# Sliding-window attention and a hard-swish MLP on one core: batch 0's values loaded by heads, w_out whole ahead of batch 1, seven units ahead of its stage

## The chip, the cores and the metric

The kernel runs on one core of a Trainium2 chip. A core has TensorE (PE in the profile; its weight loads are PEld), VectorE (DVE), ScalarE (ACT), GpSimd (POOL) and SyncE (SP); they run side by side and wait for one another by semaphores. DMAs are issued by POOL or SP and move data between the chip's memory (HBM) and the on-chip memory SBUF. PE writes to PSUM, eight banks of 2 KB a partition. The metric is the device time of one execution in microseconds; a profiled execution gives a span from the first to the last instruction, and some time lies around it.

## The reference

For 8 batches, 8 heads, 576 positions and a head size of 64, causal attention over a window of 64 positions; then, with the heads side by side as 512 columns and all batches as 4608 rows, an MLP with hidden size 2048:

```
scores = q @ k.T / 8                      # masked to 0 <= i - j < 64
attn   = softmax(scores);  o = attn @ v
x      = o as (4608, 512)
h      = x @ w_in                          # (4608, 2048)
g      = h * clip(h + 3, 0, 6) / 6
out    = g @ w_out                         # (4608, 512), float32
```

All inputs are float32 in HBM; the kernel computes in bf16 and accumulates in float32. The loads cast to bf16 on the way.

## The kernel before

The program is written out by hand under a manual schedule: each engine executes its instructions in the order in which the code issues them, and a wait at the head of an engine's queue holds everything behind it on that engine. Semaphores are placed by the framework from the tiles read and written.

The heads are worked in pairs, so a step t stands for one pair g of one batch b (t = 4b + g). Per pair the kernel transposes q and k on PE, copies them out of PSUM (KT for the keys, QZ or Q for the queries), forms scores, takes exp on ACT, multiplies with the values (P·V), scales by the reciprocals of the sums, transposes the result and copies it into xT, the left operand of the MLP. The MLP runs over blocks of 512 rows: 16 "first units" (fc 0 to 15, four matmuls with w_in each, one for each pair, L485; then ACT L497 and DVE L498 make gT) and 16 "second units" (four matmuls with w_out each, L521; four units make 128 rows of the output, copied by ACT at L527 and stored by SP).

Batch 0 has a path of its own, the head of the program:
- load_early_qk (L107) loads q and k pair by pair; load_early_v (L126) loads the values in five pieces of 128 rows with all heads (the last has 64 rows). Both are issued by POOL, which also sets up the identity and the window masks (window, late_windows) and issues w_in (three parts: fc 0 to 3, 4 to 7, 8 to 15, L163), w_out (two halves, L169), batch 1's q and k (L118) and its values (L137).
- t_k and t_q transpose a pair's keys and queries, 12 PE instructions each. The keys are copied by DVE (L239), the queries half by ACT and half by DVE (L231). The DVE half waits for the ACT half.
- s0_ makes a pair's scores with the mask added on PE (L248, L251), in three PSUM tiles of the pool ps_t, which has three banks; ACT takes the exp of each (L259 twice, L265).
- Vs is the value tile shifted by 64 rows; shift_early(m) makes it from Vn, two copies for each piece m of 128 rows, the first two pieces on POOL and the others on DVE (L150, L152).
- pv_early is P·V, 20 matmuls (L354), then a reciprocal (L363) and a product (L364) on DVE into opg. x_early transposes opg on PE (L375, five, into a tile of ps_t) and ACT copies it to xT (L378).
- warm issues matmuls on zeros that nothing reads.
- The first units of block 0 begin before all pairs are there: u(fc, gs) does the matmuls of the pairs gs and keeps the bank half way; inputs does so for several fc; complete adds the last pair and finishes fc 0 to 4.

After the head, the rest of block 0's first units runs (44 matmuls of the remaining fc), and then the 16 second units of block 0 are used as filling work: weave(n) executes the next n units of the queue moe. Between them stands batch 1's front: turn_two(4) and then, for t = 4 to 7, turn (36 transposes, L276), s_first and s_rest (scores), and weights (exp on ACT, product with the window on DVE). Then come pv and pv_out of t = 4 to 7, x_turned, batch 2's first loads, turn_two(8) and the first units of block 1. From batch 2 on a regular loop (group) weaves the MLP units between the attention steps.

POOL's DMAs use eight completion semaphores in turn, so the issue of a DMA waits until the eighth DMA before it has landed.

Of the kernel before, what the change touches and what calls it, by code (L numbers as in the profile page):

```python
# [24 lines left out]
P = 128  # L25
D = 64
W = 64
# [9 lines left out]
def kernel(  # L37
# [60 lines left out]
    def load_early_qk(pairs, first=0):  # L98
        if first:
            tiles = staged[0]  # L100
        else:
            both = stage.tile([SP, 2, H, R * D], BF16, name="qk6", tag="qk")
            tiles = [both[:, 0], both[:, 1]]
        h = 2 * first
        for n in pairs:
            for t, src in zip(tiles, (q, k)):
                nc.gpsimd.dma_start(  # L107
                    out=t[:, h : h + 2 * n, :],
                    in_=src[0, h : h + 2 * n].rearrange("h (p r) d -> p h (r d)", r=R),
                )  # L110
            h += 2 * n
        return tiles

    def load_qk(b, n=NG, first=0):
        t = staged[b] if first else stage.tile([P, H, RL * D], BF16, name="qk9", tag="qk")
        hs = slice(2 * first, 2 * (first + n))
        for z, src in enumerate((k, q)):
            nc.gpsimd.dma_start(  # L118
                out=t[halves[z], hs], in_=src[b, hs].rearrange("h (p r) d -> p h (r d)", r=RL)
            )  # L120
        return t

    def load_early_v():
        for m in range(NM):
            n = min(P, S - m * P)
            nc.gpsimd.dma_start(  # L126
                out=Vn[0][:n, m, :, 0:D], in_=v[0, :, m * P : m * P + n, :].rearrange("h s d -> s h d"),
            )

    def load_v(b, whole=False, part=slice(None)):  # L130
# [13 lines left out]
            memset(t[:, :, :, 0:VO], 1.0)  # L144
            memset(t[:, :, :, VO + P : VW], 1.0)

    def shift_early(m, move):

        vn, vs = Vn[0], Vs[0]
        move(out=vs[W:P, m], in_=vn[0:W, m])  # L150
        if m + 1 < NM:
            move(out=vs[0:W, m + 1], in_=vn[W:P, m])  # L152

    def shift(b):

# [4 lines left out]
    def load_w_in(i):  # L160
        n = FF // 4
        c = (slice(0, n), slice(n, 2 * n), slice(2 * n, FF))[i]
        nc.gpsimd.dma_start(  # L163
            out=win16[:, :, c], in_=moe_w_in[:, c].rearrange("(g p) f -> p g f", p=P)
        )

    def load_w_out(c):
        n = NFC // 2
        nc.gpsimd.dma_start(  # L169
            out=wout16[:, c * n : (c + 1) * n, :],  # L170
            in_=moe_w_out[c * n * P : (c + 1) * n * P, :].rearrange("(c p) j -> p c j", p=P),
        )
# [13 lines left out]
    def window():  # L186

        for sign, base in ((-1, -1), (1, W)):
            nc.gpsimd.affine_select(
                out=outside[:], in_=outside[:], pattern=[[sign, W]], compare_op=ISGE,  # L190
                fill=-BIG, base=base, channel_multiplier=-sign,
            )
# [15 lines left out]
    def zero_rows(i):  # L208
        nc.vector.memset(KT[i][:, 0:W], 0.0)
        nc.vector.memset(QZ[i][D:P, 0, :], 0.0)  # L210
        nc.vector.memset(QZ[i][0:D, 1, :], 0.0)
# [32 lines left out]
    def s0_(t):  # L244

        kt, qz = KT[t % 4], QZ[t % 4]
        def window_scores(to, w):
            nc.tensor.matmul(  # L248
                to, lhsT=ident[:], rhs=outside[:].unsqueeze(1).to_broadcast([P, 2, W]), start=True, stop=False
            )  # L250
            nc.tensor.matmul(  # L251
                to, lhsT=kt[:, w * W : w * W + P], rhs=qz[:, :, w * W : (w + 1) * W], start=False, stop=True
            )

        for a in range(2):
            sc = ps_t.tile([P, 2, NM - 1, W], F32, name="sc", tag="bk")
            for m in range(NM - 1):
                window_scores(sc[:, :, m], 2 * m + a)
            nc.scalar.activation(  # L259
                out=Pz[t % 4][:, :, :, a].rearrange("p h m w -> p (h m) w"),  # L260
                in_=sc[:].rearrange("p h m w -> p (h m) w"), func=EXP, scale=scale,
            )
        sl = ps_t.tile([P, 2, W], F32, name="sl", tag="bk")
        window_scores(sl[:], NW - 1)
        nc.scalar.activation(out=Pl[t % 4][:, :, 0:W], in_=sl[:], func=EXP, scale=scale)  # L265
# [73 lines left out]
    def pv_early(t):  # L339
        b, g = divmod(t, NG)  # L340
        vn, vs, pz, pl = Vn[b % 2], Vs[b % 2], Pz[t % 4], Pl[t % 4]
        if t in (1, 3):
            os = [ps_h.tile([P, 1, 512], F32, name="oh", tag="bk") for _ in range(2)]
        else:
            os = [ps_o.tile([P, 2, 512], F32, name="o", tag="o")]
        n = len(os)
        for h in range(2):
            hh = 2 * g + h
            o = os[h % n][:, h // n]
            for m in range(NM):  # L350
                om = o[:, m * (D + 1) : (m + 1) * (D + 1)]
                for a in range(2):
                    last = m == NM - 1
                    nc.tensor.matmul(  # L354
                        om[a * W : (a + 1) * W], lhsT=pl[:, h, a * W : (a + 1) * W] if last else pz[:, h, m, a, :],
                        rhs=(vn if a and not last else vs)[:, m, hh, 0 : D + 1], start=True, stop=True,
                    )
        opg = work.tile([P, NM, 2, D], BF16, name="opg")
        for i, o in enumerate(os):
            hs = slice(i, i + 2 // n)  # L360
            ov = o[:, :, 0 : NM * (D + 1)].rearrange("p h (m c) -> p h m c", c=D + 1)
            rec = recs[:, t, hs, 0:NM]
            nc.vector.reciprocal(out=rec.unsqueeze(3), in_=ov[:, :, :, D : D + 1])  # L363
            nc.vector.tensor_tensor(  # L364
                out=opg[:, :, hs].rearrange("p m h d -> p h m d"), in0=ov[:, :, :, 0:D],
                in1=rec.unsqueeze(3).to_broadcast([P, 2 // n, NM, D]), op=MULT,
            )
        opgs[t] = opg
# [202 lines left out]
    def weave(n):  # L571
        for _ in range(min(n, len(moe))):
            moe.popleft()()
# [98 lines left out]
    )  # L672
    load_early_qk((1,), 1)
    window()
    load_early_qk((1,) * (NG - 2), 2)
    zero_rows(0)
    nc.vector.memset(Vn[0][:, :, :, D:VC], 1.0)
    nc.vector.memset(band[:], 1.0)
    nc.vector.memset(first[:], 1.0)
    pads(1, nc.vector.memset)  # L680
    load_early_v()
    nc.vector.memset(Vs[0][0:W, 0], 0.0)
    for i in range(2):
        load_w_in(i)
    for m in range(2):
        shift_early(m, nc.gpsimd.tensor_copy)
    load_w_in(2)
    late_windows()
    load_w_out(0)
    staged[1] = load_qk(1, 2)  # L690
    load_w_out(1)
    load_qk(1, 2, 2)
    load_v(1, True)
    nc.vector.memset(recs[:], 1.0)
# [14 lines left out]
    t_q(1)  # L709
    zero_rows(3)  # L710
    s0_(0)
    t_k(2)
    t_q(2)
    s0_(1)
    t_k(3)
    t_q(3)
    s0_(2)
    for m in range(2, NM):
        shift_early(m, nc.vector.tensor_copy)
    s0_(3)  # L720
    warm(ps_acc, 4)
    pv_early(0)
    pv_early(1)
    warm(ps_acc, 2)
    x_early(0)
    pv_early(2)
    queue_block(0, 0)
    u = units[0][0]

    def inputs(gs, fcs, **to):  # L730
        for fc in fcs:
            u(fc, gs, **to)

    u(0, (0,), ps_acc)
    inputs((0,), (1, 2), pool=ps_t)
    x_early(1)
    pv_early(3)
    x_early(2)
    inputs((1,), range(3))
    for fc, to in zip((3, 4), pair_bank()):  # L740
        u(fc, (0, 1), to=to)
    x_early(3)
    inputs((2,), range(5))
    complete(0, range(5), (3, 4))
    def group(t, n):

        if t >= 2 * NG:
            pv(t)
        if t + 2 < T:
            turn(t + 2)  # L750
        if t + 1 < T:
            host = t + 2
            if host >= T:
                hosts[host] = [ps_h.tile([P, 8 * P], BF16, name=name, tag="bk") for name in ("tk", "tq")]
            s = s_first(t + 1, host)
            weights(t + 1, s, s_rest(t + 1))
        if t >= 2 * NG:
            pv_out(t)
        if t + 2 < T:
            turned(t + 2, 0)  # L760
        if t >= 2 * NG:
            x_(t)
        weave(2)
        if t + 2 < T:
            turned(t + 2, 1)
        weave(n - 2)
# [16 lines left out]
    n = NG  # L783
# [6 lines left out]
            (3, 0), (3, 1), (3, 2), (3, 3),  # L790
        )
    )
    weave(2)
    turn_two(n)
    weave(2)
    for t in range(n, n + 4):
        if t < n + 3:
            turn(t + 1)
        s = s_first(t, min(t + 1, n + 3))

        def copies():
            if t < n + 3:
                turned(t + 1, 0)
                turned(t + 1, 1)

        weights(t, s, s_rest(t), own, copies)
        if t < n + 3:
            weave((4, 2, 2)[t - n])
    nc.gpsimd.tensor_copy(out=seen[:], in_=P0[(n + 3) % 4][0:1, 0, 0, 0:1])
    staged[2] = load_qk(2, 1)  # L810
    for t in range(n, n + 4):
# [82 lines left out]
```

## Time and profile before

| what | value |
|---|---|
| median of 3 runs | 322.94 us (322.43 to 323.59) |
| profiled execution | 323.23 us, span 321.5 us |
| busy in the span | PE 307.6 us (96%), ACT 183.9 (57%), DVE 177.6 (55%), POOL 125.3 (39%) |
| granted TensorE clock, mean | 0.993 |
| HBM read and written | 37.62 and 9.44 MB |
| PE busy, 5 to 10, 10 to 15, 15 to 20, 20 to 25 us | 3.82, 4.34, 4.14, 4.42 of 5.00 us each |
| PE busy, 25 to 45 us | 20.00 of 20.00 us |
| DMA, 15 to 30 us | 208 GB/s |

Times in the profile's lines are microseconds from the span's start, then the duration; "L126" is line 126 of the kernel; "x5" counts instructions; a bracket names the idle time of the engine just before and what ended it. In the groups the columns are busy time and the mean duration of one in ns, then idle time before them and its main releaser. A busy PE is not PE at its peak: matmuls overlap in the pipeline, and a 128x512 one that lasts 379 ns is followed by the next after 216 ns.

### The profile page before, as it was taken

How to read it: one execution, taken by the hardware profiler on the slowest of the kernel's cores; microseconds unless marked ns; L12 is line 12 of the kernel's file. 1: busy time of each engine (PE TensorE's matmuls, PEld its weight loads, DVE VectorE, ACT ScalarE, POOL GpSimd, SP SyncE). 2: the span in 40 equal slices, each digit the busy share in tenths (PEclk: the TensorE clock that was granted, in tenths of full speed). 3: DMA queues.
4: the chain of work that ended last, by engine and by line, in shares of the span. 5: the costliest groups of instructions: out<-in, count | busy, mean ns of one | idle time of the engine just before them, and what ended most of it. 6: DMA issues, size and time to landing. Idle time of an engine off the chain costs nothing.

```text
span 321.5 us, 11140 instructions
## 1 busy us (share of the span) xinstructions
PE 307.6 (96%) x4824; PEld 156.0 (49%) x4824; DVE 177.6 (55%) x385; ACT 183.9 (57%) x345; POOL 125.3 (39%) x171
## 2 busy tenths in 40 slices
PE   7889999999989999999999999999999999999992
PEld 3744454545544555555555555555544444444440
DVE  7876757488446743775377527762676156334200
ACT  2737665598457764776477547763774356455310
POOL 8991204587866335553455335633330000000000
PEclk9999999999999999999999999999999999999997
DMA  6999995979979942994299349933022200100021
GB/s 86 169 211 206 208 184 112 220 103 115 198 103 167 123 117 86 164 130 117 87 157 136 108 97 149 147 102 103 6 62 42 86 33 0 65 35 34 34 74 66
DMA packets 57592, 35.67 MB, mean 111 GB/s; under 512 B 39872, under 2 KB 51648, under 8 KB 57536
## 3 DMA queue, kind: packets, MB, share of 16 engines
q0 software_dynamic: 35904, 18.81, 45.1%
q1 hardware_dynamic: 21632, 16.08, 21.2%
q8 instruction: 39, 0.64, 0.8%
q14 instruction: 17, 0.14, 0.1%
HBM read 37.62 MB, written 9.44 MB: 146 GB/s over the span
## 4 chain that ended last, share of the span: by engine, by line
PE 87%; ACT 3%; DVE 2%; POOL 2%; DMA 2%; issue 2%; POOLq 0%; ACTq 0%; DVEq 0%
PE hT L485 37%; PE acc L521 37%; PE o L403 4%; PE s L310 2%; PE acco L521 2%; DMA V<-in_v_dram 2%; PE tk L276 2%; POOL qk L107 2%; ACT t L497 1%; DVE gT L498 1%; PE tq L276 1%; POOL V L126 1%; PE hTo L485 1%; PE xp L375 0%; ACT e L323 0%
## 5 line engine op out<-in xcount | busy, mean ns | idle before, releaser
L498 DVE SCALAR_TENSOR_TENSOR gT<-t,hT 128x512 bf16<-128x512 bf16 x141 | 95.8, 687 | 82.7 <-ACT t L497 82.2
L485 PE MATMUL hT<-xT,win 128*128 128x512 bf16 x564 | 133.2, 379 | 1.5 <-DVE gT L498 0.6
L521 PE MATMUL acc<-wout,gT 128*128 128x512 bf16 x544 | 129.1, 379 | 0.0
L497 ACT ACTIVATE t<-hT,half_const 128x512 bf16<-128x512 f32 x141 | 95.8, 689 | 51.1 <-PE hT L485 50.5
L485 PEld LDWEIGHTS <-win 128*128 128x128 bf16 x576 | 55.8, 98 | 67.6 <-issue 2.6
L521 PEld LDWEIGHTS <-gT 128*128 128x128 bf16 x576 | 54.3, 98 | 62.8
L331 POOL TENSOR_TENSOR Pz<-e,band 128x512 bf16<-128x512 bf16 x48 | 54.1, 1145 | 0.0
L328 POOL TENSOR_TENSOR P<-e,first 64x256 bf16<-64x256 bf16 x24 | 15.9, 662 | 86.8 <-ACT e L319 86.8
L527 ACT COPY osb<-acc 128x512 f32<-128x512 f32 x34 | 19.9, 586 | 43.9 <-PE acc L521 41.1
L323 ACT ACTIVATE e<-s 128x512 bf16<-128x512 f32 x56 | 30.1, 592 | 0.0
L283 DVE COPY KT<-tk 128x576 bf16<-128x576 bf16 x28 | 20.8, 743 | 5.3 <-ACT e L319 4.5
L137 POOL DMA_DIRECT2D V<-in_v_dram x22 | 18.0, 821 | 8.3 <-DMA wout<-in_moe_w_out_dram 4.2
L412 DVE TENSOR_REDUCE sums<-o 128x12 f32<-128x24 f32 x26 | 4.6, 179 | 27.6 <-PE o L403 27.6
L403 PEld LDWEIGHTS <-Pz 64*64 64x64 bf16 x1120 | 13.5, 108 | 13.0 <-issue 11.6
L426 DVE TENSOR_TENSOR opl<-o,recs 128x256 bf16<-128x256 f32 x52 | 19.2, 406 | 0.0
L283 ACT COPY QZ<-tq 128x576 bf16<-128x576 bf16 x28 | 17.8, 637 | 1.5 <-PE tq L276 1.5
L403 PE MATMUL o<-V,Pz 64*64 64x65 bf16 x1040 | 15.5, 195 | 0.8 <-issue 0.8
L319 ACT ACTIVATE e<-tk 64x128 bf16<-64x128 f32 x28 | 7.6, 270 | 13.9 <-PE tq L296 13.9
L310 PE MATMUL s<-QZ,KT 64*64 64x64 bf16 x896 | 14.4, 195 | 0.4 <-DVE gT L498 0.4
L276 PE MATMUL tk<-ident,qk 64*64 64x64 bf16 x504 | 13.9, 195 | 0.0
L276 PE MATMUL tq<-ident,qk 64*64 64x64 bf16 x504 | 13.9, 195 | 0.0
L276 PEld LDWEIGHTS <-qk 64*64 64x64 bf16 x1008 | 11.5, 106 | 2.3 <-issue 2.1
(102 smaller groups left out, 209.0 us busy)
## 6 DMA issues: line engine op xcount, KB each, us to landing
out_dram<-osb SPq DMA_DIRECT2D x36, 256.0 KB, 2.2
V<-in_v_dram POOLq DMA_DIRECT2D x16, 256.0 KB, 6.2
V<-V SPq DMA_DIRECT2D x6, 432.0 KB, 5.0
qk<-in_k_dram POOLq DMA_DIRECT2D x4, 576.0 KB, 6.4
qk<-in_q_dram POOLq DMA_DIRECT2D x4, 576.0 KB, 9.2
wout<-in_moe_w_out_dram POOLq DMA_DIRECT2D x2, 1024.0 KB, 15.6
qk<-in_q_dram POOLq DMA_DIRECT2D x12, 144.0 KB, 4.5
qk<-in_k_dram POOLq DMA_DIRECT2D x12, 144.0 KB, 4.3
```

The source lines that it names most:

```text
L276: nc.tensor.transpose(out=hosts[t][z][halves[h], r * W : (r + 1) * W], in_=staged[b][halves[z], 2 * g + h, r * D : (r + 1) * D], identity= ...
L283: (nc.scalar.copy if z else nc.vector.tensor_copy)(out=(QZ[t % 4][:, 0] if z else KT[t % 4][:, W:]).rearrange("q (p r) -> q p r", r=RL), i ...
L310: nc.tensor.matmul(ss[h][halves[i], c, m, r], lhsT=keys(t, h, W * (w - 1), r), rhs=QZ[t % 4][halves[h], 0, w * W : (w + 1) * W], start=Tru ...
L323: nc.scalar.activation(out=e[:].rearrange("p c m r w -> p (c m r w)"), in_=ss[h][:].rearrange("p c m r w -> p (c m r w)"), func=EXP, scale ...
L331: muls[h].tensor_tensor(out=Pw[t % 4][:, h].rearrange("p c m r w -> p (c m) (r w)"), in0=e[:].rearrange("p c m r w -> p (c m) (r w)"), in1 ...
L403: nc.tensor.matmul(o[i][halves[c], c0 : c0 + D + 1], lhsT=p, rhs=vt[:, 2 * g + h, v0 : v0 + D + 1], start=(r == 0), stop=(r == 1), skip_gr ...
L426: nc.vector.tensor_tensor(out=opg[:, :, i], in0=ov[i][:, 2:6, 1 : D + 1].rearrange("p (m h) d -> p m h d", h=2), in1=rec[:, i, 2:6].rearra ...
L485: nc.tensor.matmul(hT, lhsT=win16[:, g, fc * P : (fc + 1) * P], rhs=xT[:, g, t0 : t0 + TB], start=(g == 0), stop=(g == NG - 1),)
L497: nc.scalar.activation(out=t1[:], in_=hT, func=RELU, bias=half_const[:], scale=1.0 / 6.0)
L498: nc.vector.scalar_tensor_tensor(out=gT[:, fc, :], in0=t1[:], scalar=1.0, in1=hT, op0=MIN, op1=MULT)
L521: nc.tensor.matmul(acc, lhsT=gT[:, fc, ts * P : (ts + 1) * P], rhs=wout16[:, fc, :], start=(fc == 0), stop=(fc == NFC - 1),)
L527: nc.scalar.copy(out=osb[:], in_=acc)
```

## The change

Batch 0's values are loaded by heads: load_early_v(heads) issues one DMA for each head given, with the rows 0 to 511 in four groups of 128, and load_early_v() one DMA for the last 64 rows of all heads. On POOL the order is now q and k of pairs 0 and 1, the window selects, the values of heads 0 to 3, the tail, q and k of pairs 2 and 3, the values of heads 4 to 7, the three parts of w_in, the late window selects, both halves of w_out, batch 1's q and k, its values. The number of DMAs for the values goes from five to nine.

shift_early takes a pair in place of a piece of rows: two copies of 64 partitions with 720 and 576 columns for each pair, pairs 0 and 2 on DVE, pairs 1 and 3 on ACT, none on POOL.

The order of the head becomes: transposes 0 and 1, scores 0, scores 1, shifts 0 and 1, P·V 0, transposes 2, P·V 1, scores 2, x_early 0, transposes 3, x_early 1, scores 3, shifts 2 and 3, P·V 2 and 3, x_early 2, and then the first units for fc 0 to 4 with pairs 0 and 1 together, pair 2, x_early 3 and the rest. Six warm matmuls go. P·V of pair 1 uses the pool ps_o in place of ps_h.

Of block 0's second units seven are executed before turn_two(4), one behind it, two, two and one in batch 1's rounds; before it was two, two and four, two, two. The three between the P·V steps stay, and the one that was left behind turn_two(8) is used up earlier.

```diff
@@ -120,11 +120,15 @@
             )
         return t
 
-    def load_early_v():
-        for m in range(NM):
-            n = min(P, S - m * P)
+    def load_early_v(heads=()):
+        whole = S - S % P
+        for h in heads:
             nc.gpsimd.dma_start(
-                out=Vn[0][:n, m, :, 0:D], in_=v[0, :, m * P : m * P + n, :].rearrange("h s d -> s h d"),
+                out=Vn[0][:, 0 : NM - 1, h, 0:D], in_=v[0, h, 0:whole].rearrange("(m p) d -> p m d", p=P)
+            )
+        if not heads:
+            nc.gpsimd.dma_start(
+                out=Vn[0][0 : S - whole, NM - 1, :, 0:D], in_=v[0, :, whole:S].rearrange("h s d -> s h d")
             )
 
     def load_v(b, whole=False, part=slice(None)):
@@ -144,12 +148,12 @@
             memset(t[:, :, :, 0:VO], 1.0)
             memset(t[:, :, :, VO + P : VW], 1.0)
 
-    def shift_early(m, move):
+    def shift_early(g, move):
 
         vn, vs = Vn[0], Vs[0]
-        move(out=vs[W:P, m], in_=vn[0:W, m])
-        if m + 1 < NM:
-            move(out=vs[0:W, m + 1], in_=vn[W:P, m])
+        hs = slice(2 * g, 2 * g + 2)
+        move(out=vs[W:P, :, hs], in_=vn[0:W, :, hs])
+        move(out=vs[0:W, 1:NM, hs], in_=vn[W:P, 0 : NM - 1, hs])
 
     def shift(b):
 
@@ -339,7 +343,7 @@
     def pv_early(t):
         b, g = divmod(t, NG)
         vn, vs, pz, pl = Vn[b % 2], Vs[b % 2], Pz[t % 4], Pl[t % 4]
-        if t in (1, 3):
+        if t == 3:
             os = [ps_h.tile([P, 1, 512], F32, name="oh", tag="bk") for _ in range(2)]
         else:
             os = [ps_o.tile([P, 2, 512], F32, name="o", tag="o")]
@@ -672,23 +676,22 @@
     )
     load_early_qk((1,), 1)
     window()
+    load_early_v(range(NG))
+    load_early_v()
     load_early_qk((1,) * (NG - 2), 2)
+    load_early_v(range(NG, H))
     zero_rows(0)
     nc.vector.memset(Vn[0][:, :, :, D:VC], 1.0)
     nc.vector.memset(band[:], 1.0)
     nc.vector.memset(first[:], 1.0)
     pads(1, nc.vector.memset)
-    load_early_v()
     nc.vector.memset(Vs[0][0:W, 0], 0.0)
-    for i in range(2):
+    for i in range(3):
         load_w_in(i)
-    for m in range(2):
-        shift_early(m, nc.gpsimd.tensor_copy)
-    load_w_in(2)
     late_windows()
     load_w_out(0)
+    load_w_out(1)
     staged[1] = load_qk(1, 2)
-    load_w_out(1)
     load_qk(1, 2, 2)
     load_v(1, True)
     nc.vector.memset(recs[:], 1.0)
@@ -709,21 +712,24 @@
     t_q(1)
     zero_rows(3)
     s0_(0)
+    s0_(1)
+    shift_early(0, nc.vector.tensor_copy)
+    shift_early(1, nc.scalar.copy)
+    pv_early(0)
     t_k(2)
     t_q(2)
-    s0_(1)
+    pv_early(1)
+    s0_(2)
+    x_early(0)
     t_k(3)
     t_q(3)
-    s0_(2)
-    for m in range(2, NM):
-        shift_early(m, nc.vector.tensor_copy)
+    x_early(1)
     s0_(3)
-    warm(ps_acc, 4)
-    pv_early(0)
-    pv_early(1)
-    warm(ps_acc, 2)
-    x_early(0)
+    shift_early(2, nc.vector.tensor_copy)
+    shift_early(3, nc.scalar.copy)
     pv_early(2)
+    pv_early(3)
+    x_early(2)
     queue_block(0, 0)
     u = units[0][0]
 
@@ -731,17 +737,15 @@
         for fc in fcs:
             u(fc, gs, **to)
 
-    u(0, (0,), ps_acc)
-    inputs((0,), (1, 2), pool=ps_t)
-    x_early(1)
-    pv_early(3)
-    x_early(2)
-    inputs((1,), range(3))
+    u(0, (0, 1), ps_acc)
+    inputs((0, 1), (1, 2), pool=ps_t)
     for fc, to in zip((3, 4), pair_bank()):
         u(fc, (0, 1), to=to)
+    inputs((2,), range(3))
     x_early(3)
-    inputs((2,), range(5))
+    inputs((2,), (3, 4))
     complete(0, range(5), (3, 4))
+
     def group(t, n):
 
         if t >= 2 * NG:
@@ -790,9 +794,9 @@
             (3, 0), (3, 1), (3, 2), (3, 3),
         )
     )
-    weave(2)
+    weave(7)
     turn_two(n)
-    weave(2)
+    weave(1)
     for t in range(n, n + 4):
         if t < n + 3:
             turn(t + 1)
@@ -805,7 +809,7 @@
 
         weights(t, s, s_rest(t), own, copies)
         if t < n + 3:
-            weave((4, 2, 2)[t - n])
+            weave((2, 2, 1)[t - n])
     nc.gpsimd.tensor_copy(out=seen[:], in_=P0[(n + 3) % 4][0:1, 0, 0, 0:1])
     staged[2] = load_qk(2, 1)
     for t in range(n, n + 4):
```

## The prediction

> **What bounds the kernel now.** I read the page first (shares, chain, groups), then the chain in order of time, then the timelines of the engines over the first 26 us, then the landing of each early DMA, last a table of busy time by stretch.
>
> ```profile
> PE 87%; ACT 3%; DVE 2%; POOL 2%; DMA 2%; issue 2%; POOLq 0%; ACTq 0%; DVEq 0%
> L485 PE MATMUL hT<-xT,win 128*128 128x512 bf16 x564 | 133.2, 379 | 1.5 <-DVE gT L498 0.6
> ```
>
> PE carries 87% of the chain and the big matmuls hardly wait. A change can only gain where PE is not yet dense, and it loses whatever delays the point from which PE is dense. The chain in order of time gives that point:
>
> ```profile
> 9.21 5.97 DMA V<-in_v_dram
> ...
> 16.31 0.60 DVE V L150
> ...
> 17.72 0.39 PE o L354 x11
> ...
> 19.76 0.65 ACT xT L378
> ...
> 26.66 9.50 PE hT L485 x44
> 36.15 1.73 PE acc L521 x8
> ```
>
> So today the head waits for batch 0's values (landed at 15.2), shifts them, runs the first P·V at 17.7, and from about 25.4 PE is dense: the 44 matmuls L485 end at 36.1, 0.216 us each. In the PE timeline the first matmul with w_in stands at 20.45 and the first L521 at 35.99; I count in those starts.
>
> What the head consists of, from the timelines of ACT, DVE and POOL:
>
> ```profile
> 9.88 1.08 ACT L259 ACTIVATE Pz<-sc 128x512 bf16<-128x512 f32 x2
> 10.85 0.29 ACT L265 ACTIVATE Pl<-sl 128x128 bf16<-128x128 f32 x1
> 14.11 0.76 DVE L231 COPY QZ<-tp 64x576 bf16<-64x576 bf16 x1
> 15.28 0.30 DVE L150 COPY V<-V 64x576 bf16<-64x576 bf16 x1 [0.41 <-DMA V<-in_v_dram]
> 15.62 0.66 DVE L152 COPY V<-V 64x576 bf16<-64x576 bf16 x1
> 18.39 0.82 DVE L364 TENSOR_TENSOR opg<-o,recs 128x640 bf16<-128x640 f32 x1
> 19.76 0.64 ACT L378 COPY xT<-xp 128x576 bf16<-128x576 bf16 x1 [3.00 <-PE xp L375]
> 7.45 4.22 POOL L126 DMA_DIRECT2D V<-in_v_dram  x5
> 26.57 0.88 POOL L137 DMA_DIRECT2D V<-in_v_dram  x1 [2.67 <-DMA win<-in_moe_w_in_dram]
> ```
>
> Today all four pairs' scores are finished (last L265 ends at 16.76) before the values are usable. Scores hide behind the load of V.
>
> **The change, step by step.**
>
> *Loads.* After the two window selects POOL is free at 5.0. Today q and k of pairs 2 and 3 follow (0.63 us each). Now four value loads (heads 0 to 3), the tail of 64 rows, those q and k, and four more value loads. One value load has 512 runs, like the tail of today, which took 0.73 (the whole ones 0.90). Heads 0 to 3 are issued from 5.0 to 7.92, the tail from 7.92, q2 8.65, k2 9.28, q3 9.91, k3 10.54, heads 4 to 7 from 11.2, w_in from 14.1 (11.6 today). Landing takes 3.4 (first) to 4.7 for q and k and 5.2 to 6.0 for V; I take 4.4, as of the q that now stands fifth, since the queue is less full. The tail lands at 12.3, k2 at 13.7, k3 at 14.9, heads 6 and 7 by 17.8. Each of these DMAs waits for the eighth before it (the 26.57 row is such a wait, on the third w_in load); all those have landed in time. w_in's first part lands at about 20.1 instead of 18.6, the second at 22.7 (21.2), the third at 27.8 (26.3); w_out whole at 37.7 (39.5), batch 1's q and k at 40.5 and 43.3 (34.6 and 42.5), its values near 48 either way. SP issues nothing here.
>
> *Head.* PE, ACT and DVE each keep the written order, and the order now interleaves scores and P·V. Scores 0 stay where they are; scores 1 move up and end on ACT at 12.8. From there, by the rows above:
> - DVE shifts pair 0 (720 and 576 columns) once the tail is there. A 576-column copy took 0.30 alone and 0.60 to 0.66 beside POOL, so 0.7 to 1.5 for two; POOL issues throughout, I take 1.0: 12.35 to 13.35.
> - P·V 0 on PE 0.55 (13.9); reciprocal and product on DVE 1.07 (18.14 to 19.21 today): 15.0.
> - Transposes of pair 2 stand behind P·V 0 on PE (14.65). Their two DVE copies (0.76 each) stand behind the product: 15.0 to 16.55. Today they ended at 13.29.
> - Scores 2 start at 16.6; today's scores 0 needed 1.13 from their first use of Q to the first exp's end and 1.85 to the last. The first exp ends at 17.75 and frees the bank that x_early(0) waits for; pair 3's transposes are queued behind it, to 18.75, though k3 landed at 14.9.
> - ACT finishes the last exp (18.45), copies xT 0 (0.6) and half of Q 3 (0.6): 19.65. DVE's half, which waits for it, ends at 20.45 (14.87 today).
> - Scores 3: 20.5, last exp at 22.35. Only then ACT shifts pair 3, two copies of about 0.65 (as L231, 0.63): 23.65. No row has ACT on this copy; 1.0 to 1.6 is the bound by L378 and L265 rates.
> - P·V 3 0.55, five transposes 0.27: the first matmul with w_in at 24.55 instead of 20.45.
>
> Ahead of dense PE then stand ten matmuls (2.16) and three (0.65), five transposes (0.27, 27.6), xT 3 on ACT (28.35, two matmuls beside it), five (1.08), then the 44 (9.50): L521 starts at 39.0 instead of 35.99. **+3.0 us.** The six warm-up matmuls that go (about 1.3 us) stood in waits and give nothing back. Copies that leave POOL (2.8 us) free a queue that holds nobody here. All weights are there in time (fc 8 is reached at 32.0, its weights landed at 27.8), so late loads cost nothing.
>
> *Batch 1's front.* Today from 35.99 to the first P·V of pair 4 (50.38) 14.4 us hold 12 units of w_out. Now 7 units (6.2), turn (0.41), one unit (0.9), and three rounds of turn and scores (0.74) with 2, 2 and 1 units (1.83, 1.83, 0.9). With one unit in the third round PE is through at 14.3 after the start, while ACT still copies Q 7 (osb 0.58, e 0.43, Q 0.63 after e 1.09): scores 7 begin at 14.55 and P·V 4 at 15.55. That is 1.16 longer with one unit more done (0.87): **+0.3**, bounds 0 and 0.6. At the end no unit is left behind turn(8); xT 6 is copied meanwhile and the first three matmuls use pairs 4, 5 first, so 0 to 0.1.
>
> *Sum.* +3.0 and +0.3 make +3.3. From 60 us on PE is dense and nothing gives it back: loads of batch 2 are issued behind PE's own progress. The profiled execution took 323.23 (span 321.5 and 1.7 around it), 0.29 above the median of 322.94. The profiled one would take 326.5, the median **326.2 us**. By the ends: a landing 3.4 after issue, a shift of 0.7 and no loss in the front give +2.1 (the DVE's memsets until 11.71 stop it there), a landing of 5.4, a shift of 1.5 and ACT copies of 1.6 give +5.1: 325.0 to 328.0 for this case.
>
> **A rule beside the row.** PE now has gaps of 1.0 to 1.7 us at 12, 15.6, 19.1 and 22.1, and is about half idle from 12 to 24.5. The end of the run shows the clock falling:
>
> ```profile
> 314.00:316.00 2.00, 1.28 (x6) 0.39 (x4) 0.00 (x0) 0.58 (x1) 0.00 (x0) 1.00 0.06 18
> 316.00:318.00 2.00, 0.00 (x0) 0.00 (x0) 0.00 (x0) 0.00 (x0) 0.00 (x0) 0.83 0.38 139
> 318.00:320.00 2.00, 0.00 (x0) 0.00 (x0) 0.00 (x0) 0.00 (x0) 0.00 (x0) 0.50 0.02 8
> ```
>
> The columns behind the width are PE, weight loads, DVE, ACT, POOL, then the granted clock. The last matmul ends at 315.3; 0.83 over 316 to 318 means that half clock began near 317.3, 2 us later. The gaps above are all under 2 us, so the sum has full clock.
>
> The Trainium skill, "TensorE: Matmul & The Clock Gate", Part 1, says that the clock halves after an idle window of about 3.4 us. By that the sum would be the same, but the row falls sooner than the page says, and the rule speaks against removing warm-up matmuls.
>
> **The rivals.**
> - *The clock falls in the gaps* (the kernel is slower still). For it: half-idle PE and dummies removed; against it: no single gap reaches 2 us, and today the clock stays at 1.00 through waits of 0.3 to 1.2. At the start the matmuls ran 0.43 apart from 1.26 to 5.5 before they ran 0.216 apart, so 4.2 us at half speed, 2.1 lost: 328.3, up to 330 with a late fall.
> - *Faster: V arrives early enough and the interleaved head runs ahead.* It decides at a first w_in matmul of 21.25 (24.55 less 3.3); at 20.3 it would reach fc 8 when its weights land (27.8), and 8 x 0.864 puts the first L521 at 34.7, 1.3 earlier, less 0.3: 321.9. For it: pairs 0 and 1 finish P·V some 3 to 4 us earlier. Against it: scores 3 depend on transposes written behind x_early(0), a chain of 12 us from the tail's landing, which must lose 3.3.
> - *No change*: the chain is shorter by half of that and batch 1's front loses nothing; 322.9 to 324.
>
> **How the numbers follow.** Head chain as summed 0.68, clock 0.14, faster 0.10, in between 0.08, of which 0.05 lies within 0.3% (0.97 us, about what a measurement can tell here). Slower is 0.68 + 0.14 + 0.03 = 0.85, same 0.05, faster 0.10. The range runs from inside the in-between case, 323.7, to above the clock case, 328.9, leaving out the faster case and the tails.
>
> **What would show it.** Right: the last L231 copy on DVE ends near 20.5, the last L259/L265 exp near 22.3, the first w_in matmul near 24.5, the first L521 near 39.0, P·V 4 near 54.5, no wait of PE on w_in or w_out. Wrong: a first w_in matmul before 22; PE waiting for a w_in load; L485 spaced 0.43 apart; ACT's shift far from 1.3; or PE gaining behind 60 us.

## The result, and the profile after

The changed kernel takes 327.52 us in the median of four executions (326.80 to 328.48), the kernel before 322.69 (322.25 to 323.59) beside it. The ratio is 1.0133 with a 95% interval of 1.0096 to 1.0170: slower by 3.1 to 5.5 us. The forecast was 326.2 and slower; the time lies in its range, 1.3 above the forecast. The profiled execution took 327.19 with a span of 325.5, 4.0 over the 321.5 of before, where the sum had said 3.3. (Of the profiles further down, unit_back's is of a slow execution, 331.37 us, which its ratio leaves out; of it only the clock and the places of its waits are read.)

The page's chain and groups, after (lines of the code are 4 higher than before from L130 on):

```profile
PE 86%; DMA 3%; ACT 3%; issue 2%; POOL 2%; DVE 1%; SPq 0%; POOLq 0%; ACTq 0%
L489 PE MATMUL hT<-xT,win 128*128 128x512 bf16 x551 | 131.6, 379 | 1.2 <-ACT xT L382 0.3
```

The big matmuls are as long as before (379 ns) and still hardly wait. What changed is the point from which PE is dense. The chain in order of time (start, duration, what):

```profile
7.96 0.70 POOL V L130
...
9.25 3.77 DMA qk<-in_k_dram
...
15.65 0.11 PE sc L255
...
17.25 0.53 PE xp L379 x5
17.79 1.08 PE tp L225 x24
...
19.55 0.77 DVE QZ L235
...
20.64 0.06 PE sc L255
...
22.23 0.79 ACT V L155
...
23.05 0.68 ACT V L156
...
24.68 1.24 PE hT L489 x5
...
39.17 1.73 PE acc L525 x8
```

The values are out of the chain except for their issue. It now goes through k of pair 2 (landed at 13.0), its copies and scores, x_early(0), pair 3's transposes (17.79), the copy of Q 3 (19.55), scores 3, and ACT's shift of pair 3, to the first matmul with w_in at 24.68. The first L525 starts at 39.01 (35.99 before), the first P·V of pair 4 at 54.50.

Two of these rows look wrong beside their neighbours. Scores 2 run 0.11 apart at 15.65, scores 3 run 0.06 apart at 20.64; pair 3's transposes take 1.08, while pair 2's set of 24, at 13.06 of the same chain, took 0.72. The table by stretch (PE, weight loads, DVE, ACT, POOL, granted clock, DMA) says why:

```profile
14.00:16.00 2.00, 1.27 (x29) 1.18 (x27) 1.86 (x4) 0.43 (x1) 1.67 (x3) 0.81 2.01 154
16.00:18.00 2.00, 2.00 (x25) 1.80 (x25) 0.34 (x1) 1.52 (x4) 1.63 (x5) 0.50 1.30 147
18.00:20.00 2.00, 1.28 (x30) 1.13 (x25) 1.21 (x2) 1.57 (x3) 1.93 (x5) 0.84 1.23 203
```

The granted clock was half from about 15.3 to 18.7. Before the change it was 1.00 in each stretch from 10 to 30 us.

Behind the head, PE's timeline has waits that the old kernel does not have:

```profile
56.03 0.19 PE L407 MATMUL ot<-V,P 64*64 64x65 bf16 x1 [0.82 <-issue]
67.39 0.21 PE L280 MATMUL tk<-ident,qk 64*64 64x64 bf16 x1 [0.87 <-DMA qk<-in_k_dram]
68.10 0.21 PE L280 MATMUL tq<-ident,qk 64*64 64x64 bf16 x1 [0.49 <-DMA qk<-in_q_dram]
73.18 0.42 PE L407 MATMUL o<-V,Pz 64*64 64x65 bf16 x29 [0.57 <-DMA V<-V]
```

The rows at 67.39 and 68.10 are q and k of batch 2's second pair, wanted 0.87 sooner against the attention steps because no unit of w_out is left behind turn_two(8). The row at 56.03 has no semaphore behind it; the old profile has such a stall too:

```profile
89.78 0.23 PE L403 MATMUL o<-V,Pz 64*64 64x65 bf16 x5 [0.85 <-issue]
```

So the account of the 4.0 us is: 3.02 at the first L525; 3.25 at P·V 4 (4.12 later, with one unit of 0.87 more done); 0.82 for the stall at 56.03; about 0.5 for q and k (1.36 waited, less the 0.87 of the unit); together 4.6. Read at the copies of Q (L283 before, L287 after, the same pair in both kernels), the changed kernel is 4.4 to 4.8 behind from the third pair of batch 2 on, 4.4 behind once the old kernel has had its own stall of 0.85, and 4.0 from 110 us to the end, behind another of 0.36 in the old one at 101.6.

### The profile page after: what moved, and what is told of

It reads as the page before. It is cut to its first block, busy times and chain, and to the rows that moved or that the text cites. A ratio compares the mean times of both kernels' runs of the same rounds, so it can differ in the third digit from the quotient of the medians.

```text
span 325.5 us, 11093 instructions
## 1 busy us (share of the span) xinstructions
PE 304.2 (93%) x4777; PEld 156.8 (48%) x4818; DVE 176.8 (54%) x382; ACT 186.8 (57%) x349; POOL 125.1 (38%) x171
## 4 chain that ended last, share of the span: by engine, by line
PE 86%; DMA 3%; ACT 3%; issue 2%; POOL 2%; DVE 1%; SPq 0%; POOLq 0%; ACTq 0%
PE acc L525 36%; PE hT L489 35%; PE o L407 4%; PE s L314 2%; PE acco L525 2%; DMA V<-V 2%; PE tk L280 2%; DMA qk<-in_k_dram 1%; POOL qk L107 1%; POOL V L126 1%; PE tq L280 1%; DVE gT L502 1%; PE tp L225 1%; PE sc L255 0%; DVE QZ L235 0%
## 5 line engine op out<-in xcount | busy, mean ns | idle before, releaser
L489 PE MATMUL hT<-xT,win 128*128 128x512 bf16 x551 | 131.6, 379 | 1.2 <-ACT xT L382 0.3
L525 PE MATMUL acc<-wout,gT 128*128 128x512 bf16 x518 | 125.8, 379 | 2.5 <-issue 1.6
L525 PEld LDWEIGHTS <-gT 128*128 128x128 bf16 x576 | 54.4, 98 | 63.0
L287 DVE COPY KT<-tk 128x576 bf16<-128x576 bf16 x28 | 20.8, 743 | 7.1 <-PE tq L280 5.1
L287 ACT COPY QZ<-tq 128x576 bf16<-128x576 bf16 x28 | 17.8, 637 | 5.8 <-PE tq L280 5.8
```

Of the source, the lines that this page charges most:

```text
L287: (nc.scalar.copy if z else nc.vector.tensor_copy)(out=(QZ[t % 4][:, 0] if z else KT[t % 4][:, W:]).rearrange("q (p r) -> q p r", r=RL), i ...
L489: nc.tensor.matmul(hT, lhsT=win16[:, g, fc * P : (fc + 1) * P], rhs=xT[:, g, t0 : t0 + TB], start=(g == 0), stop=(g == NG - 1),)
L525: nc.tensor.matmul(acc, lhsT=gT[:, fc, ts * P : (ts + 1) * P], rhs=wout16[:, fc, :], start=(fc == 0), stop=(fc == NFC - 1),)
```

## The experiments

My theory was that the head is set by the order of its steps, that the clock stays up, and that batch 1's front costs little. The rivals were the clock, and a larger loss behind the head. Each ratio below is to the kernel before on the same chip; its medians there lay between 322.6 and 323.8. None of the kernels changes what is computed.

**The two halves of the change apart.** new_head is the changed kernel with the old order of w_out and the old units; new_tail is the reverse.

new_head, against the changed kernel:

```diff
-    load_w_out(1)
     staged[1] = load_qk(1, 2)
+    load_w_out(1)
...
-    weave(7)
+    weave(2)
     turn_two(n)
-    weave(1)
+    weave(2)
...
-            weave((2, 2, 1)[t - n])
+            weave((4, 2, 2)[t - n])
```

new_tail, against the kernel before:

```diff
     load_w_out(0)
-    staged[1] = load_qk(1, 2)
     load_w_out(1)
+    staged[1] = load_qk(1, 2)
...
-    weave(2)
+    weave(7)
     turn_two(n)
-    weave(2)
+    weave(1)
...
-            weave((4, 2, 2)[t - n])
+            weave((2, 2, 1)[t - n])
```

> The head of the changed kernel (values by heads, interleaved order, shifts by pairs) with the old order of w_out and the old numbers of units (2, 2, then 4, 2, 2). Theory A (the written order of the head is a chain that ends 3 us later, and the rest comes from the second half of the change): first L521 near 39.0 as in the changed kernel, time 2.7 to 3.3 us above the kernel before, 325.4 to 326.0. Rival B (the head costs the whole 4.8 us, also by later DMAs): 327 to 328.

> The old head with w_out whole ahead of batch 1's queries and keys, seven units ahead of the stage and one, two, two, one in it. Theory A with the forecast's price for batch 1's front alone: +0.3, 323.0. Theory A with the lost cover (no unit behind the transposes of pair 0 of batch 2, so that PE arrives 0.87 us earlier at transposes whose load has not landed, and again at the shifted values): +1.0 to +1.8, 323.7 to 324.5, with a wait of PE on a load of qk between 60 and 66 us. Rival B: 322.7, no loss.

new_head: ratio 1.0139 (1.0078 to 1.0201), first matmul with w_in at 25.25, first L525 at 39.58, span 324.8 (+3.3). new_tail: ratio 1.0039 (1.0009 to 1.0068), first L521 at 36.25, span 321.8 (+0.3). Most of the loss is the head's. How much, the times and the profile do not say alike: by the times new_head loses 2.5 to 6.5 us, and its median of 327.42 lies where rival B had it, while its profile shows the 3.3 of theory A. The tail alone costs 0.3 to 2.2 us by the times; its own profile shows 0.3, with a wait of 0.57 for a q of batch 2 at 64.43, such as the second case of theory A named. In new_head the clock fell too (0.50 over 16 to 18), and its head is 0.57 longer than the changed kernel's.

**The clock held up.** warm_gaps adds 14 matmuls on zeros in the changed kernel's waits.

```diff
     pv_early(0)
+    warm(ps_acc, 2)
     t_k(2)
     t_q(2)
     pv_early(1)
+    warm(ps_acc, 3)
     s0_(2)
...
     x_early(1)
+    warm(ps_acc, 4)
     s0_(3)
...
     pv_early(2)
+    warm(ps_acc, 5)
     pv_early(3)
```

> The changed kernel with 14 matmuls on zeros in the gaps of the head (2 behind P.V 0, 3 behind P.V 1, 4 ahead of scores 3, 5 behind P.V 2). If the half clock from 15.3 to 18.7 us is on the chain of the head: full clock there, scores 2, x_early 0 and transposes 3 take 2.1 instead of 3.6 us, first matmul with w_in at 23.2 to 23.6 instead of 24.68, time 1.0 to 1.4 us below the changed kernel. If the clock explains the whole loss of the head (rival C): 3 us below, at the kernel before plus 1. If the copies on ACT and DVE cover it: no difference, or up to 0.3 above because a dummy stands ahead of real work.

```profile
14.00:16.00 2.00, 1.88 (x48) 1.43 (x48) 1.84 (x3) 0.63 (x1) 2.00 (x4) 1.00 1.86 150
16.00:18.00 2.00, 1.81 (x34) 1.47 (x34) 1.17 (x3) 1.23 (x4) 1.80 (x6) 1.00 1.43 159
```

The clock is 1.00 where it was 0.81 and 0.50. Yet the first matmul with w_in comes at 24.11, only 0.57 sooner, and the first L525 at 38.65, 0.36 sooner. But in this run pair 0's shift took 1.45 instead of 0.79, and scores 2 began 0.90 later, at 16.18. From the first product of scores 2 to that of scores 3 it needed 3.83 us, where the changed kernel needed 5.08:

```profile
15.28 0.27 PE L255 MATMUL sc<-QZ,KT 128*128 128x128 bf16 x1 [0.73 <-DVE QZ L235]
...
20.36 0.22 PE L255 MATMUL sc<-QZ,KT 128*128 128x128 bf16 x1 [1.08 <-DVE QZ L235]
```

The ratio is 1.0143 (1.0096 to 1.0190): no gain that the times show. It is not that the clock was up in the profile alone: the mean granted clock has a median of 0.997 over the eight executions of warm_gaps, and it was 0.990 to 0.993 in the four of the changed kernel. A fall of one such stretch costs the head about 1.1 us (lead_six below); the larger part of the head's loss stays with the clock up.

**The order of the head.** order3 is the changed kernel with pair 3's transposes ahead of x_early(0), and pairs 2 and 3 shifted on DVE ahead of scores 3.

```diff
-    x_early(0)
     t_k(3)
     t_q(3)
+    x_early(0)
     x_early(1)
-    s0_(3)
     shift_early(2, nc.vector.tensor_copy)
-    shift_early(3, nc.scalar.copy)
+    shift_early(3, nc.vector.tensor_copy)
+    s0_(3)
```

> The changed kernel with the transposes of pair 3 ahead of x_early 0, and both shifts of pairs 2 and 3 on DVE ahead of scores 3. Same loads. Theory A (order, not loads, sets the head): scores 3 start at 18.8 instead of 20.4, P.V 3 no longer waits for ACT, first matmul with w_in at 22.4 instead of 24.7, first matmul with w_out at 36.7 instead of 39.0: 2.0 to 2.5 us below the changed kernel. Rival (the later q, k and values of pairs 2 and 3 set it): less than 0.7 us below.

In PE's timeline of order3:

```profile
19.25 0.22 PE L255 MATMUL sc<-QZ,KT 128*128 128x128 bf16 x1 [0.80 <-DVE QZ L235]
...
51.34 0.19 PE L280 MATMUL tk<-ident,qk 64*64 64x64 bf16 x1 [1.25 <-issue]
```

With the same loads, the head is 2.01 shorter (first L525 at 37.00). But the clock stayed at 1.00 here, so part of this is the clock. The fair neighbour is lead_six (below), which has the changed kernel's head, the clock at 1.00, and scores 2 beginning at the same time (16.00, here 15.99): its first L525 comes at 38.47, 1.5 later. So the place of pair 3's steps, with its shift on DVE instead of ACT, costs 1.5 of the 2.5 that the head loses with the clock up; these edits were not tried apart. What makes up the other 1.0 was not tried either; in order3 DVE is busy for 7.11 of the 8 us from 14 to 22. The whole is shorter in the profile (span 323.9, 1.6 less), but not by the times: ratio 1.0125 (1.0065 to 1.0185). P·V 4 starts at 53.81, only 0.69 sooner, since 1.25 went in a stall in the middle of pair 7's transposes that no semaphore explains.

order3_old_tail is order3 with the old order of w_out and the old units (as in new_head).

> The changed kernel's loads, with the transposes of pair 3 ahead of x_early(0) and the shifts of pairs 2 and 3 on DVE ahead of scores 3 (as in the earlier run order3, whose first L521 came at 37.0), and with the old order of w_out and batch 1's q and k and the old weaves. Theory (the two parts of the change cost separately: the head by its order, batch 1's front by its weaves and loads): first L521 at 37.0, no wait of batch 1's transposes on q and k (order3 had 2.3 us there), and a span about 1.0 us above the kernel before: 322.2 to 323.0 against 321.5. Rival (a gain in the head is given back later, whatever stands there): first L521 at 37.0 but a span of 324 or more.

The first L525 is at 37.06, as expected, and at the copies of Q the kernel stays 1.1 to 1.3 behind the one before until 82 us. The ratio is 1.0062 (1.0036 to 1.0088), against order3's 1.0125: about 2 us less, at the edge of what the intervals tell. From new_head it differs by order3's edit alone, and there the ratio was 1.0139 (from 1.0078): about 2.5 us less, again with intervals that just overlap. The span of its profile is 325.2, and this is why (PE's waits):

```profile
PE hT L489 <- DMA xT<-opg: 2.0, 1, 2.0
```

Up to 95.6 PE waits 2.04 for a DMA transpose, and from 96.0 the clock is at 0.50 for about 3.4 us. The expectation is wrong in one point: what I had counted in order3 as waits of batch 1's transposes for q and k are 0.81 for the DMAs of batch 2's second pair, the stall above, and one of 0.42 at 77.6, which no DMA explains. The rival, a gain that is given back wherever it stands, came true in this profile and not in the times.

**A unit put back, and loads released sooner.** These tell what the missing unit behind turn_two(8) costs.

unit_back:

```diff
-            weave((2, 2, 1)[t - n])
+            weave((2, 2, 0)[t - n])
```

loads_sooner:

```diff
-    nc.gpsimd.tensor_copy(out=seen[:], in_=P0[(n + 3) % 4][0:1, 0, 0, 0:1])
+    nc.gpsimd.tensor_copy(out=seen[:], in_=P0[(n + 2) % 4][0:1, 0, 0, 0:1])
...
-        behind(t)
+        behind(max(t - 1, n))
```

lead_six:

```diff
-    weave(7)
+    weave(6)
```

> The changed kernel, with no unit of w_out in batch 1's third round, so that one unit stands behind turn_two(8) again, as before the change. Its trace has PE waiting 0.87 and 0.49 us for q and k of batch 2's second pair and 0.57 for a shifted value, behind turn_two(8), and a lead of the old kernel that grows there. Theory (lost cover): with about 0.9 us of PE work put back in front, the waits on that q and k shrink from 1.4 to about 0.5 or less, P.V 4 starts some 0.3 to 0.9 earlier than 54.5, and the whole is 0.3 to 1.2 us shorter than the changed kernel: a span of 324.3 to 325.2 against 325.5. Rival (the transfers are late by the queue, whatever PE does): the landing moves with PE, the waits stay at 1.2 or more, and the span is within 0.3 of 325.5.

> The changed kernel with batch 2's loads on POOL released one step sooner: the first behind the weights of t = 6 in place of t = 7, the later ones behind the product of the pair before. In the changed kernel PE waited 0.87 and 0.49 us for q and k of batch 2's second pair (issued 61.1 and 61.7, landed 6.2 and 6.4 later) and 0.57 for a shifted value, since no unit of w_out is left behind turn_two(8). unit_back put a unit back there and lost 0.9 us to a copy of keys in batch 1's third round. Theory (lost cover costs about 1 us, and only because the loads are late): with the loads some 1.5 to 2.5 us sooner these waits shrink to below 0.4 in total, the lead over the kernel before stays at or below what it is at P.V 4, and the whole is 0.5 to 1.2 us below the changed kernel's. Rival (other transfers, now in the way of these or of the output's stores, take it back): waits of the same size elsewhere, time within 0.3 us of the changed kernel's.

> The changed kernel with six units ahead of turn_two(4) in place of seven, so that one unit stands behind turn_two(8), as before the change. unit_back took that unit from batch 1's third round, where it covered a copy of keys (0.90 us of waiting); loads_sooner issued batch 2's q and k only 0.55 sooner against PE. Theory (lost cover): from the first L525 to P.V 4 PE needs 0.87 less, the two waits for q and k of batch 2's second pair (0.87 and 0.49 in the changed kernel) together fall below 0.6, and what the kernel loses between P.V 4 and the end, at equal work and without stalls that no semaphore explains, falls by about 0.5; a time 0.3 to 0.7 us below the changed kernel's, which the comparison of times can hardly show. Rival (the transfers come as late as PE lets them, since they are released by PE's own progress): the two waits stay at 1.2 or more in total, with a unit between them or not.

unit_back: ratio 1.0127 (1.0086 to 1.0167), equal to the changed kernel's. The waits for q and k are gone, and 0.90 for a copy of keys (DVE) came in batch 1's third round. loads_sooner: 1.0168 (1.0129 to 1.0207). Its edit did little: the copy ahead of the value loads waited 1.82 on POOL for pair 4's product, so the q and k in question were issued only 0.55 sooner against PE, and PE still waited 0.93 and 0.74. lead_six: 1.0173 (1.0129 to 1.0217). No wait for q and k of batch 2 is left in its profile, so these two waits are the lost unit's. But the unit that went from the front opened another wait there (PE's timeline), and the DMA transpose came late again:

```profile
50.71 1.02 PE L525 MATMUL acco<-wout,gT 128*128 128x512 bf16 x4 [1.25 <-ACT osb L531]
...
98.93 1.24 PE L489 MATMUL hT<-xT,win 128*128 128x512 bf16 x5 [2.04 <-DMA xT<-opg]
```

For the waits the theory holds and the rival does not: they vanish with the unit between. For the time the theory does not hold: it is not shorter.

The heads of these three are the changed kernel's, and they show what the clock can do to it. In lead_six it stayed at 1.00, with the same code, and the first L525 came at 38.47:

```profile
16.00 0.22 PE L255 MATMUL sc<-QZ,KT 128*128 128x128 bf16 x1 [0.69 <-DVE QZ L235]
...
19.82 0.22 PE L255 MATMUL sc<-QZ,KT 128*128 128x128 bf16 x1 [1.08 <-DVE QZ L235]
```

In new_head scores 2 began at 15.99, the clock was down for one stretch of 3.4 us, and the first L525 came 1.11 later, at 39.58; that is the price of one fall. In loads_sooner it was down from about 9.5 and again from 16.4, for 3.4 us each: 40.22. In unit_back's profile it stayed down from about 14 to 31 us, and the first L525 came at 43.36:

```profile
26.00:30.00 4.00, 4.00 (x14) 1.77 (x15) 1.05 (x3) 0.64 (x1) 0.45 (x1) 0.50 1.14 186
```

**The warm matmuls.** no_warm is the kernel before without the six that the change removes.

```diff
-    warm(ps_acc, 4)
     pv_early(0)
     pv_early(1)
-    warm(ps_acc, 2)
     x_early(0)
```

> The kernel before without the six warm matmuls that the change removes (four ahead of P.V 0, two ahead of x_early 0); nothing else changes. Theory that the six kept the clock up: the granted clock falls to about half somewhere between 17 and 22 us for some 3.4 us, as it does in the changed kernel at 15.3 to 18.7, and the first L521 comes 0.5 to 2 us behind 35.99. Theory that they only stood in waits, as the prediction says: clock 1.00 throughout, first L521 at 36.0 within 0.3, and a span within 0.3 of the kernel before.

```profile
16.00:18.00 2.00, 0.78 (x19) 0.47 (x21) 1.68 (x4) 0.71 (x3) 1.80 (x6) 1.00 1.24 206
18.00:20.00 2.00, 1.38 (x37) 1.09 (x30) 1.67 (x5) 0.00 (x0) 1.93 (x5) 0.51 1.24 207
...
22.00:24.00 2.00, 1.97 (x31) 1.66 (x30) 0.69 (x3) 0.64 (x1) 2.00 (x3) 0.50 1.11 209
```

The clock fell for 6.8 us and the first L521 came at 37.89, 1.90 late. So the six did keep the clock up in the old head. It is not this profile's alone: the mean granted clock has a median of 0.9905 over the ten executions of no_warm, and of 0.995 over the 27 of the kernel before beside them. The span is 322.6 (+1.1), the ratio 1.0008 (0.9980 to 1.0035): what a profile shows of this does not show in the times of ten executions.

**Could the old head be shortened?** pair_shift takes only the shift by pairs into the kernel before; pair_split spreads the pairs over three engines.

In both, shift_early copies a pair, as in the changed kernel, and the pieces' copies on POOL are gone. pair_shift:

```diff
-    for m in range(2, NM):
-        shift_early(m, nc.vector.tensor_copy)
+    shift_early(0, nc.vector.tensor_copy)
+    shift_early(1, nc.vector.tensor_copy)
     s0_(3)
+    shift_early(2, nc.scalar.copy)
+    shift_early(3, nc.scalar.copy)
```

pair_split, against pair_shift:

```diff
     staged[1] = load_qk(1, 2)
+    shift_early(3, nc.gpsimd.tensor_copy)
...
-    shift_early(1, nc.vector.tensor_copy)
     s0_(3)
-    shift_early(2, nc.scalar.copy)
-    shift_early(3, nc.scalar.copy)
+    shift_early(1, nc.scalar.copy)
     warm(ps_acc, 4)
     pv_early(0)
-    pv_early(1)
+    shift_early(2, nc.vector.tensor_copy)
     warm(ps_acc, 2)
+    pv_early(1)
```

> The kernel before, in which only the shift of batch 0's values changes: by pairs in place of by pieces of rows, pairs 0 and 1 on DVE ahead of scores 3, pairs 2 and 3 on ACT behind the exps of scores 3, and none on POOL. Loads and the order of everything else are the old ones. Theory (the head's length is set by the order of the steps, and by the wait for the last shift): the first P.V needs one pair's two copies in place of all pieces, P.V 0 starts about 1 us before 17.7, pair 3's transposes of the result come at about 22.6 in place of 24.05, the first L521 at about 34.6 to 35.0 in place of 35.99, and the span is 1.0 to 1.5 us below the kernel before. Rival (ACT is the next to be late): the four copies of about 0.7 us on ACT stand ahead of the copy of xT 0, the first matmul with w_in comes 1 us or more behind 20.45, and the span is equal or up to 1 us longer.

> The kernel before with batch 0's values shifted by pairs, as in pair_shift, but each pair's two copies where its engine has room: pair 0 on DVE ahead of scores 3, pair 1 on ACT behind the exps of scores 3, pair 2 on DVE behind P.V 0's product, pair 3 on POOL behind batch 1's first q and k; the two warm matmuls stand between P.V 0 and P.V 1. In pair_shift P.V 0's reciprocal waited on DVE behind pair 1's copies (18.08 in place of about 17.5), and ACT was taken up to 19.70. Theory (what counts in the head is what stands ahead of P.V 0's product and of the first copy of xT on its engine): the reciprocal comes at about 17.5, x_early(0) at 18.6 in place of 19.27, the first matmul with w_in at 19.8 in place of 20.45, the first L521 at 35.4 in place of 35.99, and the span is 0.4 to 0.7 us below the kernel before. Rival (the last piece of the values, landing at 16.2, bounds the head whatever the copies do): first L521 within 0.2 of 35.99 and the same time. Rival (the copies on POOL and ACT slow DVE's): first matmul with w_in behind 20.45, up to 0.5 longer.

pair_shift: first L521 at 35.93 instead of 34.6 to 35.0, span 321.3, ratio 0.9987 (0.9963 to 1.0012). Its DVE timeline shows where the expected 1 us went:

```profile
16.30 0.52 DVE L151 COPY V<-V 64x720 bf16<-64x720 bf16 x1 [1.51 <-DMA V<-in_v_dram]
...
18.08 0.22 DVE L363 RECIPROCAL recs<-o 128x10 f32<-128x10 f32 x1
```

A pair's copy needs all five pieces of the values, and the last landed by 16.3 (16.16 in pair_split); the copies by pieces start at 13.21 and 15.28 as pieces land. pair_split has the reciprocal at 17.73, 0.4 sooner than the kernel before, but pair 2's copies took 0.86 and 0.68 on DVE, the first beside POOL's copies of pair 3 (0.52 and 0.30 for the same forms in pair_shift's first pair). P·V 2 waited 0.93 for them, and the first L521 came at 36.62. Its ratio is 1.0026 (0.9995 to 1.0057). The second rival, slower copies on DVE, fits this; that POOL's copies are the cause was not tried apart. The same DMA transpose held PE up for 2.04 here. Neither beats the kernel before.

## Why the prediction was right

*The head, +3.0: right in place, and in size by some luck.* First matmul with w_in 24.68 (24.55 forecast), first L525 39.01 (39.0). The chain runs through the steps that were named: transposes 3 behind x_early(0), DVE's half of Q 3 (ended 20.31, forecast 20.45), scores 3 at 20.36 (20.5), ACT's shift to 23.72 (23.65). ACT's two copies took 0.79 and 0.68, inside the 1.0 to 1.6 for both. order3 shows that the place of pair 3's steps, and not the loads, costs 1.5 of this.

*But two errors cancelled in it.* The tail of the values was there by 11.3 (12.3 forecast), DVE's shift took 0.8 for 1.0 (in the other runs of this head it took 0.96 to 1.45), and so scores 2 started at 15.28, 1.3 ahead of the forecast:

```profile
11.30 0.38 DVE L155 COPY V<-V 64x720 bf16<-64x720 bf16 x1
11.71 0.38 DVE L156 COPY V<-V 64x576 bf16<-64x576 bf16 x1
```

Half clock gave that back: from the first of scores 2 to the first of scores 3 it took 5.08, against 3.9 in the forecast and 3.82 in lead_six, so 1.2 to 1.3. With the clock at 1.00 the head is 2.5 to 2.7 longer than before (lead_six, warm_gaps), not 3.0. Once the clock falls it is 3.0 to 4.2 (the changed kernel, new_head, loads_sooner), and 7.4 in unit_back's profile.

*"The gaps above are all under 2 us, so the sum has full clock": this step failed.* The rival that the clock falls had 0.14 and came true in the profile, at 15.3, without a single gap of 2 us. The row used for the rule, at the end of the run, showed an idle PE; it said nothing of one that is half idle. Nor do 2 us of idle PE suffice: gaps of 2.1 to 2.2 ahead of the second set of transposes (at 8.46 in new_tail, 8.54 in no_warm, 8.74 in lead_six) left the clock at 1.00. The price was wrong as well: 2.1 more was forecast and one fall costs about 1.1. The median, 327.52, lies between the likeliest case (326.2) and this rival's 328.3. The Trainium skill, "TensorE: Matmul & The Clock Gate", Part 1, speaks of a free-running window of 3413 ns. That is the length of the fall here (15.3 to 18.7), and twice it in no_warm. But its table asks for an idle window, and PE was busy for 57% of the 3.4 us before the fall, so that this row alone does not give the fall; the same Part also tells, under "A second HAM failure mode", of a clock that swings where PE is often idle for a short time between groups of matmuls, which is nearer to this head.

*"The six warm-up matmuls ... stood in waits and give nothing back": half right.* Nothing came back, but they had a use: without them alone the clock fell (no_warm).

*Batch 1's front, +0.3: right in the profile.* P·V 4 started at 54.50, as forecast. By the times the new tail alone costs 0.3 to 2.2, so 0.3 is the lower edge of what was measured.

*"At the end no unit is left behind turn(8) ... 0 to 0.1": mis-sized.* The reason looked at xT 6 only. What the unit also hid was the landing of batch 2's second q and k; their loads are released by PE's own progress, so they do not come sooner when PE does. It cost about 0.5 in the profile; with the unit back between (lead_six) these waits are gone. With the stall at 56.03 it makes 1.3, which puts the account at 4.6; the span shows 4.0, 0.7 over the sum's 3.3, since the old kernel's profile has stalls of its own (0.85 and 0.36). The stalls are in no term of the sum.

*The weights: right.* PE waited for no part of w_in or w_out, though the third load of w_in was issued 0.57 late, behind q of pair 3, which the forecast had landed in time. *Faster:* the first w_in matmul would have had to come at 21.25, and scores 3, for the reason given, started only at 20.36.

## What to carry to other kernels

When steps are interleaved on engines that keep the written order, follow the last pair through every queue: an operand that lands earlier for the first pair gains nothing if the last pair's transposes now stand behind the first pair's results. Matmuls on zeros that stand in waits can still hold the clock up, even where, as here, the times of ten executions show no loss without them; a head that is half idle should be costed with the clock up and with it down. Filling work that is taken from one place was cover there, here for a transfer, a copy of keys or a copy of the output: name what it hides before pricing its absence at nothing.

## What the runs showed of the hardware

- The granted clock fell to half in heads in which PE was 54 to 60% busy over the 3.4 us before, with no gap of 2 us there, at other times from run to run, and for 3.4, 6.8 or (unit_back's profile) about 17 us; the same head once kept 1.00 (lead_six). The busy share alone does not decide: in the changed kernel PE was 56% busy from 22.1 to 25.5, and the clock stayed at 1.00. What does is open.
- PE stalled for 0.4 to 1.75 us with no semaphore behind it, in the middle of a group of small matmuls or between large ones, at other places in eleven of the thirteen profiles (0.85 at 89.78 before, 0.82 at 56.03 after, 1.25 at 51.34 in order3, 1.75 at 104.89 in warm_gaps). They may be a part of the spread of 3 to 6 us between executions of one kernel; that was not tried, and what they are stays open.
- A DMA transpose that normally hides held PE up for 2.04 us in three profiles (order3_old_tail, pair_split, lead_six), the same amount each time, for 0.61 in order3, and not in the others. Only in order3_old_tail did the clock fall behind it. Why is open.
